# PSUM banks shared out by stage, an earlier end of the first batch's attention, and values loaded ahead of stores

## The chip, the cores and the metric

The kernel runs on one core of a Trainium2 chip. The metric is the device time of one execution in microseconds (us). Before the change three runs gave a median of 913.34 us (911.04 to 914.92).

## The reference

Three parts follow one another. q, k and v have 4 batches, 8 heads, 576 tokens and 64 dimensions. Per head there are two attentions, and their results are added: one over q, k, v averaged over groups of 4 tokens (144 by 144 scores), one over the full sequence in which a token sees only tokens nearer than 4.

```python
q_d, k_d, v_d = (t.reshape(B, H, 144, 4, D).mean(axis=3) for t in (q, k, v))
out_d = softmax(scale * q_d @ k_d.T) @ v_d
local = where(abs(i - j) < 4, scale * q @ k.T, -1e9)
x = repeat(out_d, 4) + softmax(local) @ v      # 2304 tokens x 512
h = x @ w_in                                   # 512 -> 2048
x = (h * sigmoid(1.702 * h)) @ w_out           # 2048 -> 512
out = ((x @ w1) * (x @ w2)) @ w3 @ w_out2      # 512 -> 1024 -> 1024 -> 512
```

## The kernel before

The large weights are loaded as 64-bit numbers and decoded to fp32 on VectorE (DVE; L176, L179 and L182) and ScalarE (ACT, L169). Every large product is made of three TensorE (PE) matmuls on a high and a low half of each operand (`mm3`, L120 to L123); the halves are made by `split` (L113 to L115: ACT writes the high half, DVE or GpSimd (POOL) the low one).

**First stage (0 to about 122 us).** w3 times w_out2 is computed once, so that the second half of the model needs one product less. There are 16 steps (two halves by 8 row tiles). Step s has a w3 tile, decoded, transposed by four PE transposes (`w34_transpose`, L624) into the one bank of the PSUM pool `psh`, and copied out of it as `w3t` by ACT (L626) and DVE (L627); then `w34_mm` issues 12 matmuls into four accumulators `ps_w34` (pool `psy`, four banks). The transposes of step s + 2 are issued ahead of the matmuls of step s.

**Attention.** A pair of heads is one unit n, 4 units a batch; here it is called a head. It has pieces: T (transposes of q and k, L286), S (scores: local ones L332, averaged ones L367, then the softmax on DVE, ACT and POOL), P (transposes of the probabilities, L417) and V (products with v, L446 and L459, then `v_pool` L452 and `v_local` L467, which adds both and stores x to DRAM, `x_d`, L471). Batch 0's pieces are woven into the first stage and batch b + 1's into block b of what follows. `att_pieces` writes the list of pieces with a gap behind each; `Pump` hands out a piece when the gap has been counted down, one count per call, and a call stands behind every `mm3` of the first stage. Banks for T, S, P and the V parts come from the pool `pst`, three banks. The softmax of batch 0 has its exps on ACT, 12 to a head (L317).

**Blocks.** The 2304 tokens go in five blocks (512, 512, 512, 256, 512 tokens). At a block's start x is read back from `x_d` (`tok_load`, L648) in four pieces and split (`tok_split`, `x_t`, L114 and L115). Then 16 steps `h_step` (12 matmuls into `ps_h`, the activation L676, a split) and `y_step` (12 matmuls into `ps_y`). The four heads of the last batch take another way for their local attention, on DVE and POOL (`l_scores` and others, L504 and on), woven into the blocks too. From the fourth block on no attention is left.

**What sets the order.** Each engine works through its own queue in order, and the order in the queue is made ahead of time by a scheduler from issue order, priorities and dependencies. `tc.issue_after(x)` only says that an instruction stands behind x in that order: an attention piece stands behind the `mm3` that came before it in the program (L609, `done["mm"]`), and may be put later. SP and ACT also issue the DMAs, each in the order of its queue.

## Time and profile before

| what | value |
|---|---|
| median of three runs | 913.34 us |
| profiled execution | 912.47 us, span 910.7 us, so 1.77 us lie outside the span |
| PE busy | 848.9 us, 93% |
| DVE busy | 598.4 us, 66% |
| ACT busy | 385.2 us, 42% |
| POOL busy | 149.6 us, 16% |

The span is the time from the first to the last instruction. Busy time is the sum in which an engine had an instruction under way; an idle time is printed in brackets behind the instruction in front of which it lies, with what ended it. In the timelines start times are microseconds from the span's start, and "x4" behind an instruction stands for four in a row. The granted clock is 1.00 for 2.4 GHz; 0.50 would be 1.2 GHz throughout.

### The profile page before, as it was taken

To read this page: it belongs to the slowest core of one execution; us is meant where nothing else is said; L and a number is where in the kernel's file an instruction comes from. 1 tells how busy PE (TensorE), PEld (TensorE's weight loads), DVE (VectorE), ACT (ScalarE), POOL (GpSimd) and SP (SyncE) were. 2 spreads that over 40 slices of the span, in tenths; PEclk is the share of its full clock that TensorE was granted. 3 is DMA by queue.
4 is the path that set the end of the run, shared out by engine and by line. 5 is a ranking of instruction groups with operands and counts; after the bars stand their busy time and mean duration, and the time that the engine had idled before them with its cause. 6 is when DMAs were issued, how large, how long until landed. Compare 5 with 4: busy or idle time off the path is not lost.

```text
span 910.7 us, 13574 instructions
## 1 busy us (share of the span) xinstructions
PE 848.9 (93%) x5132; PEld 721.9 (79%) x5132; DVE 598.4 (66%) x1061; ACT 385.2 (42%) x748; POOL 149.6 (16%) x153
## 2 busy tenths in 40 slices
PE   4497977999988999989999999999999999999998
PEld 3375865887756877767788998888999899989996
DVE  5896668898779999694446795333545554555451
ACT  4575655776534545343345665333111411141111
POOL 6642433432223432310000000000000000000000
PEclk9798987999998989989999999999999999999999
DMA  8865674665653443443334999601555455545521
GB/s 239 251 196 151 190 205 148 181 184 147 155 173 80 88 96 99 107 112 59 80 115 151 355 309 355 220 0 47 200 205 207 175 193 211 206 176 187 217 81 70
DMA packets 140598, 150.76 MB, mean 166 GB/s; under 512 B 86898, under 2 KB 121460, under 8 KB 136436
## 3 DMA queue, kind: packets, MB, share of 16 engines
q1 hardware_dynamic: 119424, 141.21, 47.9%
q10 hardware_dynamic: 21108, 8.69, 3.9%
q8 instruction: 40, 0.66, 0.3%
q14 instruction: 26, 0.21, 0.1%
HBM read 117.75 MB, written 32.11 MB: 165 GB/s over the span
## 4 chain that ended last, share of the span: by engine, by line
PE 60%; DVE 1%; ACT 1%; POOL 0%; issue 0%; ACTq 0%
PE ps_ab L123 6%; PE ps_ab L121 6%; PE ps_ab L122 6%; PE ps_y L121 5%; PE ps_y L122 5%; PE ps_y L123 5%; PE ps_h L121 5%; PE ps_h L122 5%; PE ps_h L123 5%; PE ps_o L122 4%; PE ps_o L123 4%; PE ps_o L121 4%; PE ps_pt L417 1%; PE ps_sp L367 0%; PE ps_v L459 0%; PE ps_vp L446 0%
## 5 line engine op out<-in xcount | busy, mean ns | idle before, releaser
L121 PE MATMUL ps_h<-x_t,w 128*128 128x512 f32 (+1 forms) x320 | 126.6, 395 | 14.6 <-ACT g_t L676 6.0
L122 PE MATMUL ps_h<-x_t,w 128*128 128x512 f32 (+1 forms) x320 | 123.3, 385 | 7.5 <-DVE x_t L115 7.4
L123 PE MATMUL ps_h<-x_t,w 128*128 128x512 f32 (+1 forms) x320 | 122.2, 382 | 0.0
L122 PE MATMUL ps_y<-gl,w 128*128 128x512 f32 (+1 forms) x320 | 118.9, 372 | 2.0 <-DVE gl L115 2.0
L121 PE MATMUL ps_y<-gh,w 128*128 128x512 f32 (+1 forms) x320 | 118.4, 375 | 0.0
L123 PE MATMUL ps_y<-gh,w 128*128 128x512 f32 (+1 forms) x320 | 118.2, 369 | 0.0
L123 PE MATMUL ps_ab<-b_t,a_in 128*128 128x384 f32 x336 | 112.5, 335 | 0.0
L121 PE MATMUL ps_ab<-b_t,a_in 128*128 128x384 f32 x336 | 112.5, 335 | 0.0
L122 PE MATMUL ps_ab<-b_t,a_in 128*128 128x384 f32 x336 | 112.4, 334 | 0.0
L115 DVE TENSOR_TENSOR gl<-g_t,gh 128x512 fp32r<-128x512 f32 (+1 forms) x80 | 56.7, 709 | 72.4 <-ACT gh L114 72.0
L676 ACT ACTIVATE g_t<-ps_h 128x512 f32<-128x512 f32 (+1 forms) x80 | 44.3, 554 | 130.8 <-PE ps_h L123 118.2
L121 PEld LDWEIGHTS ps_h<-x_t,w 128*128 128x128 f32 x320 | 62.4, 195 | 31.6 <-ACT g_t L676 9.9
L122 PEld LDWEIGHTS ps_h<-x_t,w 128*128 128x128 f32 x320 | 62.8, 196 | 18.6 <-DVE x_t L115 9.8
L123 PEld LDWEIGHTS ps_h<-x_t,w 128*128 128x128 f32 x320 | 62.8, 196 | 10.9
L114 ACT ACTIVATE abh<-ab 128x384 fp32r<-128x384 f32 x24 | 12.6, 526 | 137.2 <-DVE ab L801 137.2
L122 PEld LDWEIGHTS ps_y<-gl,w 128*128 128x128 f32 x320 | 60.4, 189 | 12.7 <-DVE gl L115 3.4
L121 PEld LDWEIGHTS ps_y<-gh,w 128*128 128x128 f32 x320 | 60.6, 189 | 11.0 <-issue 1.0
L123 PEld LDWEIGHTS ps_y<-gh,w 128*128 128x128 f32 x320 | 60.3, 189 | 10.0
L182 DVE SCALAR_TENSOR_TENSOR dec<-dec,st 128x512 int32<-128x512 int32 x72 | 58.1, 815 | 12.8 <-ACT dec L169 11.3
L121 PEld LDWEIGHTS ps_ab<-b_t,a_in 128*128 128x128 f32 x336 | 63.1, 188 | 0.9
L122 PEld LDWEIGHTS ps_ab<-b_t,a_in 128*128 128x128 f32 x336 | 63.1, 188 | 0.9
L123 PEld LDWEIGHTS ps_ab<-b_t,a_in 128*128 128x128 f32 x336 | 63.1, 188 | 0.0
(152 smaller groups left out, 1639.9 us busy)
## 6 DMA issues: line engine op xcount, KB each, us to landing
a_in<-a_d SPq DMA_DIRECT2D x24, 1792.0 KB
st<-in_moe_w_dram SPq DMA_DIRECT2D x32, 512.0 KB
a_d<-ap SPq DMA_DIRECT2D x8, 1792.0 KB
st<-in_moe_w_out_dram SPq DMA_DIRECT2D x24, 512.0 KB
st<-in_moe_w_in_dram SPq DMA_DIRECT2D x16, 512.0 KB
yr<-y_d SPq DMA_DIRECT2D x12, 384.0 KB
out_dram<-osb SPq DMA_DIRECT2D x17, 256.0 KB
s_v<-in_v_dram ACTq DMA_DIRECT2D x15, 288.0 KB
```

What stands on the lines that cost most here:

```text
L114: nc.scalar.activation(hi, raw, AF.Copy)
L115: lo_eng.tensor_tensor(lo, raw, f32(hi), op=ALU.subtract)
L121: nc.tensor.matmul(ps, ll, rh, start=start, stop=False, skip_group_check=more)
L122: nc.tensor.matmul(ps, lh, rl, start=False, stop=False, skip_group_check=more)
L123: done["mm"] = nc.tensor.matmul(ps, lh, rh, start=False, stop=stop, skip_group_check=more)
L182: nc.vector.scalar_tensor_tensor(t, t, 3, st[:, :, 0], op0=ALU.logical_shift_left, op1=ALU.bitwise_or)
L417: nc.tensor.transpose(ps[:, i - c0], src, ident)
L676: nc.scalar.activation(g[:, :n], ps[:, :n], AF.Gelu_apprx_sigmoid)
```

## The change

In the first stage `psh` gets two banks and `pst` two (one and three before); both pools are closed behind the stage and opened anew as `psh1` with one bank and `pst1` with three, which is what the blocks had before. In the first stage S is issued as two pieces, `s_near` (local scores, their reduction and exps) and then `s_far` (averaged scores); before, one piece had the averaged scores first. The gaps change: for batch 0 from 2 to 1 behind a piece, with a wait of 3 calls ahead of every V and 3 behind it; for later batches a wait of 6 ahead of every V and 10 behind it, where there were 16 behind V and 4 ahead of the last V alone. The rest of batch 0's attention and the first two loads of x from `x_d` are issued ahead of the 15th step's matmuls, and the rest of the loads and the splits ahead of the 16th's (before: all behind the 16th). In the blocks the `mm3` behind an attention piece is to stand behind that piece's last matmul. The loads of the next head's values (`vw`) are issued behind V's local matmuls, ahead of the two stores to `x_d`, where they stood behind them.

```diff
@@ -73,8 +73,10 @@
     dram = ctx.enter_context(tc.tile_pool(name="dram", bufs=1, space=DRAM))
     ldp = ctx.enter_context(tc.tile_pool(name="ldp", bufs=len(LOCAL), space=DRAM))
     psy = ctx.enter_context(tc.tile_pool(name="psy", bufs=1, space=PSUM))
-    psh = att_end.enter_context(tc.tile_pool(name="psh", bufs=1, space=PSUM))
-    pst = att_end.enter_context(tc.tile_pool(name="pst", bufs=3, space=PSUM))
+
+    ps_end = ctx.enter_context(ExitStack())
+    psh = ps_end.enter_context(tc.tile_pool(name="psh", bufs=2, space=PSUM))
+    pst = ps_end.enter_context(tc.tile_pool(name="pst", bufs=2, space=PSUM))
     x_d = dram.tile([128, KD, NT], F32, name="x_d")
     y_d = dram.tile([128, KD, NT], F32, name="y_d")
@@ -115,10 +117,12 @@
         lo_eng.tensor_tensor(lo, raw, f32(hi), op=ALU.subtract)
-    done = {"mm": None}
+    done = {"mm": None, "att": None, "strict": False}
     def mm3(ps, lh, ll, rh, rl, start, stop, more=False):
-        nc.tensor.matmul(ps, ll, rh, start=start, stop=False, skip_group_check=more)
+        att, done["att"] = done["att"], None
+        with tc.issue_after(att.ins) if att and done["strict"] else ExitStack():
+            nc.tensor.matmul(ps, ll, rh, start=start, stop=False, skip_group_check=more)
         nc.tensor.matmul(ps, lh, rl, start=False, stop=False, skip_group_check=more)
         done["mm"] = nc.tensor.matmul(ps, lh, rh, start=False, stop=stop, skip_group_check=more)
@@ -283,7 +287,7 @@
             halves = [pst.tile([128, FAC, UC], F32, tag="t", name="ps_t") for _ in range(2)]
             for c, ps in reversed(list(enumerate(halves))):
                 for r in range(FAC):
-                    nc.tensor.transpose(ps[:, r], st[:, c, r].rearrange("p h d -> p (h d)"), ident[:UC, :UC])
+                    done["att"] = nc.tensor.transpose(ps[:, r], st[:, c, r].rearrange("p h d -> p (h d)"), ident[:UC, :UC])
             for c, ps in enumerate(halves):
                 nc.scalar.activation(dst[:, c * UC:(c + 1) * UC].rearrange("p u r -> p r u"), ps, AF.Copy)
         if name == "q":
...
@@ -339,6 +343,19 @@
         nc.vector.tensor_reduce(at["mx", n][:, i0:i1], e[:, i0:i1], op=ALU.max, axis=X)
         if own_exp:
             s_exp(n, i0, i1, lambda i: e[:, i], SCALE)
+
+    def s_near(n, own_exp):
+        s_tiles(n, own_exp)
+        at["el", n] = att.tile([128, NQB, KW], F32, tag="el", name="el")
+        for i0, i1 in ((0, HQ), (HQ, NQB)):
+            ps = pst.tile([128, i1 - i0, KW], F32, tag="t", name="ps_s")
+            s_local_mm(n, i0, i1, ps)
+            s_local(n, i0, i1, own_exp, ps)
+
+    def s_far(n, own_exp):
+        s_pool(n, own_exp, s_pool_mm(n))
+        if n == 0:
+            v_means(0)
     def s_all(n, own_exp):
         s_tiles(n, own_exp)
@@ -355,8 +372,6 @@
         else:
             ps = s_pool_mm(n)
         s_pool(n, own_exp, ps)
-        if n == 0:
-            v_means(0)
     def s_pool_mm(n):
         kd = at["kd", n]
...
@@ -431,6 +446,8 @@
         ps = v_pool_mm(n, both[:, :SD])
         for i0, i1, pl in halves:
             v_local_mm(n, i0, i1, pl)
+        if n + 1 < B * HP and n + 1 not in LOCAL:
+            att_load_v(n + 1)
         v_pool(n, ps)
         for i0, i1, pl in halves[::-1]:
             v_local(n, i0, i1, pl)
...
@@ -469,8 +486,6 @@
             od[:, u0:u1].unsqueeze(2).to_broadcast([128, u1 - u0, FAC]), op=ALU.add)
         b, hp = divmod(n, HP)
         nc.sync.dma_start(out=x_d[:, hp, b * S + i0 * QB:b * S + i1 * QB], in_=xo)
-        if i1 == NQB and n + 1 < B * HP and n + 1 not in LOCAL:
-            att_load_v(n + 1)
     def l_load(n):
@@ -554,6 +569,8 @@
         if what == "T":
             return [lambda name=name: t_piece(n, name) for name in "qk"]
+        if what == "S" and n < HP:
+            return [lambda: s_near(n, own_exp), lambda: s_far(n, own_exp)]
         if what == "S":
             return [lambda: s_all(n, own_exp)]
         if what == "P":
@@ -562,32 +579,31 @@
             return [lambda: v_all(n), lambda: l_out(n, 0, HQ), lambda: l_out(n, HQ, NQB)]
         return [lambda: v_all(n)]
-    def att_pieces(b, own_exp, rest):
+    def att_pieces(b, own_exp):
         n0, out_ = b * HP, []
+        gap, wait, rest = (1, 3, 3) if b == 0 else (2, 6, 10)
         def add(n, what, gap):
-            fns = stage(n, what, own_exp)
-            out_.extend((fn, gap) for fn in fns)
+            out_.extend((fn, gap) for fn in stage(n, what, own_exp))
         if b == 0:
             add(n0, "T", 1)
-        add(n0, "S", 2)
-        add(n0 + 1, "T", 2)
-        out_.append((None, rest))
+        add(n0, "S", gap)
+        add(n0 + 1, "T", gap)
+        out_.append((None, wait + rest - 4))
         for i in range(HP):
             add(n0 + i, "P", 1)
             if i + 1 < HP:
-                add(n0 + i + 1, "S", 2)
+                add(n0 + i + 1, "S", gap)
                 if n0 + i + 2 < B * HP:
-                    add(n0 + i + 2, "T", 2)
-            else:
-                out_.append((None, 4))
-            add(n0 + i, "V", 2)
+                    add(n0 + i + 2, "T", gap)
+            out_.append((None, wait))
+            add(n0 + i, "V", gap)
             out_.append((None, rest))
         return out_
@@ -864,7 +880,7 @@
         jobs.size(2)
         jobs.decode(2)
         jobs.size(2)
-        pump = Pump(att_pieces(0, True, 6))
+        pump = Pump(att_pieces(0, True))
         w34_ready(0)
         pump.one()
         jobs.decode(2)
@@ -877,15 +893,22 @@
         for s, (half, j) in enumerate(steps):
             jobs.load(njobs(s + 4))
             w34_ready(s + 2)
+            if s == len(steps) - 2:
+
+                pump.drain()
+                tok_load(x_d, 0, 0)
+                tok_load(x_d, 0, 1)
+            elif s == len(steps) - 1:
+                tok_rest(x_d, 0)
             w34_mm(half, j, pump)
             jobs.decode(njobs(s + 2))
             jobs.size(njobs(s + 4))
-        pump.drain()
         early["pri"] = 100
-        tok_load(x_d, 0, 0)
-        tok_load(x_d, 0, 1)
         jobs.split(2)
-        tok_rest(x_d, 0)
+        done["strict"] = True
+        ps_end.close()
+        psh = att_end.enter_context(tc.tile_pool(name="psh1", bufs=1, space=PSUM))
+        pst = att_end.enter_context(tc.tile_pool(name="pst1", bufs=3, space=PSUM))
         def w34_load(f):
             t = g2p.tile([128, NB], F32, tag="xr", name="w34r")
@@ -920,7 +943,7 @@
         a_done = 0
         for j in range(nblk):
             last = j == nblk - 1
-            pump = Pump(att_pieces(j + 1, False, 16)) if j + 1 < B else Pump()
+            pump = Pump(att_pieces(j + 1, False)) if j + 1 < B else Pump()
             if j == nblk - 2:
                 jobs.split(2)
                 assert not jobs.jobs and not jobs.loaded and not jobs.sized and next(local, None) is None
```

The first place is PE's queue in the first stage, at the transposes of the fourth to sixth w3 tile. `ps_w<-ident,dec` are those transposes, `ps_w_297` to `ps_w_389` the four accumulators, `ps_t` is T, `ps_pt` is P, `ps_s` the local scores (the trace counts each matmul of S and V twice). Before:

```order
L122 MATMUL ps_w_389<-w,w3t 128x512
L123 MATMUL ps_w_389<-w,w3t 128x512
L624 MATMUL ps_w<-ident,dec 128x128 x4
L286 MATMUL ps_t<-ident,s_k 128x72 x4
L624 MATMUL ps_w<-ident,dec 128x128 x4
L121 MATMUL ps_w_297<-w,w3t 128x512
L122 MATMUL ps_w_297<-w,w3t 128x512
L123 MATMUL ps_w_297<-w,w3t 128x512
L417 MATMUL ps_pt<-ident,el 72x128 x8
L121 MATMUL ps_w_362<-w,w3t 128x512
```

After:

```order
L127 MATMUL ps_w_389<-w,w3t 128x512
L290 MATMUL ps_t<-ident,s_k 128x72 x8
L640 MATMUL ps_w<-ident,dec 128x128 x4
L432 MATMUL ps_pt<-ident,el 72x128 x8
L640 MATMUL ps_w<-ident,dec 128x128
L432 MATMUL ps_pt<-ident,ep 72x128 x3
L432 MATMUL ps_pt<-ident,el 72x128
L432 MATMUL ps_pt<-ident,ep 72x128 x3
L640 MATMUL ps_w<-ident,dec 128x128 x3
L336 MATMUL ps_s<-kT,qT 64x72 x18
L640 MATMUL ps_w<-ident,dec 128x128 x4
L125 MATMUL ps_w_297<-w,w3t 128x512
```

Behind the third step's matmuls stood the transposes of one w3 tile, four of T, and the transposes of the next tile; now eight of T, three tiles' transposes, all of P and the local scores of a head stand there, ahead of the fourth step's matmuls.

The second place is PE's queue at the end of the first stage, where `ps_v` is V of the batch's last head and `ps_h<-x_t` is the first work of block 0. Before:

```order
L122 MATMUL ps_w_970<-w,w3t 128x512
L123 MATMUL ps_w_970<-w,w3t 128x512
L417 MATMUL ps_pt<-ident,el 72x128
L417 MATMUL ps_pt<-ident,ep 72x128 x3
L446 MATMUL ps_v<-PT,vd 64x144 x2
L459 MATMUL ps_v<-PT,vw 64x64
L446 MATMUL ps_v<-PT,vd 64x144 x2
L459 MATMUL ps_v<-PT,vw 64x64 x17
L121 MATMUL ps_h<-x_t,w 128x512
L122 MATMUL ps_h<-x_t,w 128x512
L123 MATMUL ps_h<-x_t,w 128x512
```

After:

```order
L476 MATMUL ps_v<-PT,vw 64x64 x18
L127 MATMUL ps_w_1003<-w,w3t 128x512
L125 MATMUL ps_w_1020<-w,w3t 128x512
L126 MATMUL ps_w_1020<-w,w3t 128x512
L127 MATMUL ps_w_1020<-w,w3t 128x512
L125 MATMUL ps_w_1036<-w,w3t 128x512
L126 MATMUL ps_w_1036<-w,w3t 128x512
L127 MATMUL ps_w_1036<-w,w3t 128x512
L125 MATMUL ps_w_1080<-w,w3t 128x512
L126 MATMUL ps_w_1080<-w,w3t 128x512
L127 MATMUL ps_w_1080<-w,w3t 128x512
L125 MATMUL ps_h<-x_t,w 128x512
```

Before, V was the last work of the stage; now the last ten matmuls of the 16th step stand behind it.

The third place is DVE's queue at the start of block 1, around the splits `x_t<-xr`; `prod<-ql,kl` and `s` are the last batch's local attention, `el<-ps_s` to `el<-el,mx` the softmax of a head of batch 2. Before:

```order
L338 TENSOR_TENSOR el<-ps_s,band 128x360
L512 TENSOR_REDUCE r<-s 128x9
L339 TENSOR_REDUCE mx<-el 128x5
L513 TENSOR_TENSOR s<-s,r 128x63
L338 TENSOR_TENSOR el<-ps_s,band 128x288
L373 TENSOR_REDUCE mx<-ps_sp 128x3
L339 TENSOR_REDUCE mx<-el 128x4
L377 TENSOR_TENSOR ep<-ps_sp,mx 128x432
L515 TENSOR_REDUCE r<-s 128x9
L381 TENSOR_TENSOR el<-el,mx 128x648
L516 TENSOR_SCALAR r<-r 128x9
L115 TENSOR_TENSOR x_t<-xr,x_t 128x512
```

After:

```order
L117 TENSOR_TENSOR x_t<-xr,x_t 128x512
L521 TENSOR_REDUCE s<-prod 128x9
L117 TENSOR_TENSOR x_t<-xr,x_t 128x512
L526 TENSOR_TENSOR s<-s,near 128x63
L342 TENSOR_TENSOR el<-ps_s,band 128x360
L527 TENSOR_REDUCE r<-s 128x9
L343 TENSOR_REDUCE mx<-el 128x5
L528 TENSOR_TENSOR s<-s,r 128x63
L342 TENSOR_TENSOR el<-ps_s,band 128x288
L388 TENSOR_REDUCE mx<-ps_sp 128x3
L343 TENSOR_REDUCE mx<-el 128x4
L392 TENSOR_TENSOR ep<-ps_sp,mx 128x432
```

The block's last split stood behind seven instructions of a softmax, and stands ahead of them now.

## Rows read from the trace of the kernel before

**Rows 1.** Windows: length, busy of PE, PEld, DVE, ACT, POOL, clock, DMA.

```profile
23.00:46.00 23.00, 10.50 (x49) 8.20 (x49) 20.56 (x31) 12.20 (x37) 13.85 (x12) 0.70 0.81 250
46.00:69.00 23.00, 22.02 (x175) 17.51 (x174) 22.97 (x44) 17.69 (x49) 10.67 (x8) 0.93 0.60 189
69.00:92.00 23.00, 16.76 (x141) 13.22 (x140) 14.60 (x27) 13.02 (x42) 5.24 (x6) 0.85 0.56 164
...
138.00:161.00 23.00, 17.24 (x64) 13.19 (x64) 20.14 (x32) 13.82 (x24) 7.58 (x8) 0.78 0.45 140
...
391.00:414.00 23.00, 20.14 (x83) 14.89 (x84) 19.79 (x37) 10.58 (x17) 3.26 (x2) 0.85 0.51 129
414.00:437.00 23.00, 23.00 (x117) 18.31 (x117) 9.39 (x18) 9.09 (x14) 2.02 (x2) 1.00 0.28 53
```

**Rows 2.** Timeline of PE, 45 to 60 us: start, duration, instruction, idle before it.

```profile
45.10 1.12 PE L624 MATMUL ps_w<-ident,dec 128*128 128x128 f32 x4 [9.50 <-DVE w3t L627]
...
47.30 1.91 PE L417 MATMUL ps_pt<-ident,el 128*72 128x128 f32 x8
...
53.80 1.30 PE L332 MATMUL ps_s<-kT,qT 64*64 64x72 f32 x36
...
59.32 0.47 PE L286 MATMUL ps_t<-ident,s_q 72*128 72x72 f32 x4 [0.64 <-DVE el L338]
```

**Rows 3.** Timeline of DVE, 37 to 48 us.

```profile
37.45 1.49 DVE L176 TENSOR_SCALAR st<-st 128x512 int32<-128x512 int32 x1
...
47.32 0.42 DVE L176 TENSOR_SCALAR st<-st 128x512 int32<-128x512 int32 x1
```

**Rows 4.** Timeline of PE, 68 to 84 us.

```profile
70.15 0.39 PE L122 MATMUL ps_w<-w,w3t 128*128 128x512 f32 x1
70.38 0.39 PE L123 MATMUL ps_w<-w,w3t 128*128 128x512 f32 x1
...
74.94 0.66 PE L624 MATMUL ps_w<-ident,dec 128*128 128x128 f32 x4 [2.19 <-DVE w3t L627]
79.61 1.12 PE L624 MATMUL ps_w<-ident,dec 128*128 128x128 f32 x4 [4.01 <-DVE w3t L627]
...
83.47 0.95 PE L367 MATMUL ps_sp<-kd,qd 64*64 64x144 f32 x12
```

**Rows 5.** Timeline of DVE at 77.8 us.

```profile
77.80 0.43 DVE L176 TENSOR_SCALAR st<-st 128x512 int32<-128x512 int32 x1 [1.84 <-DMA st<-in_moe_w_in_dram]
```

**Rows 6.** Timeline of ACT, first and last of one head's 12 exps.

```profile
61.85 0.33 ACT L317 ACTIVATE el<-el,nb 128x72 f32<-128x72 f32 x1
...
66.43 0.37 ACT L317 ACTIVATE ep<-ps_sp,nb 128x144 f32<-128x144 f32 x1
```

**Rows 7.** Timeline of PE, 124 to 152 us.

```profile
124.49 1.22 PE L459 MATMUL ps_v<-PT,vw 72*64 72x64 f32 x34
...
143.57 0.80 PE L122 MATMUL ps_h<-x_t,w 128*128 128x512 f32 x1 [2.36 <-DVE x_t L115]
...
151.79 0.40 PE L121 MATMUL ps_y<-gh,w 128*128 128x512 f32 x1
```

**Rows 8.** Timeline of all engines, 131 to 143 us.

```profile
131.79 0.81 DVE L467 TENSOR_TENSOR xo<-ps_v,od 128x320 f32<-128x320 f32 x2
...
134.74 0.33 SPq L648 DMA_DIRECT2D xr<-x_d  x1
...
138.00 0.68 ACT L169 ACTIVATE dec<-st 128x512 f32<-128x512 f32 x1 [3.02 <-DMA st<-in_moe_w_out_dram]
...
140.02 0.64 ACT L114 ACTIVATE x_t<-xr 128x512 fp32r<-128x512 f32 x1
...
142.83 0.68 DVE L115 TENSOR_TENSOR x_t<-xr,x_t 128x512 fp32r<-128x512 f32 x1
```

**Rows 9.** Timeline of PE, 269 to 274 us.

```profile
269.74 0.50 PE L122 MATMUL ps_h<-x_t,w 128*128 128x512 f32 x1 [2.22 <-DVE x_t L115]
...
273.66 0.79 PE L121 MATMUL ps_h<-x_t,w 128*128 128x512 f32 x1 [1.59 <-ACT x_t L114]
```

More of the change, by code (lines that the diff above doesn't have):

```diff
@@ L331, in s_local_mm @@
                 p = slice(h * D, (h + 1) * D)
-                nc.tensor.matmul(
+                done["att"] = nc.tensor.matmul(
                     ps[p, i - i0], qT[p, i * QB:(i + 1) * QB], kT[p, w0:w0 + KW], start=True, stop=True)
@@ L366, in s_pool_mm @@
                 p = slice(h * D, (h + 1) * D)
-                nc.tensor.matmul(ps[p, j], qd[p, j * PB:j * PB + QB], kd[p], start=True, stop=True)
+                done["att"] = nc.tensor.matmul(ps[p, j], qd[p, j * PB:j * PB + QB], kd[p], start=True, stop=True)
         return ps
@@ L416, in p_piece @@
                     src = at["ep", n][:, j, kc * UC:(kc + 1) * UC]
-                nc.tensor.transpose(ps[:, i - c0], src, ident)
+                done["att"] = nc.tensor.transpose(ps[:, i - c0], src, ident)
         for c0, c1, ps in banks:
@@ L445, in v_pool_mm @@
                 i = NQB + kc * NPB - NPH
-                nc.tensor.matmul(
+                done["att"] = nc.tensor.matmul(
                     ps[p], vd[:, h, kc], PT[:, i:i + NPB, h * QB:h * QB + PB], start=kc == 0, stop=kc == 1)
@@ L458, in v_local_mm @@
                 p = slice(h * D, (h + 1) * D)
-                nc.tensor.matmul(
+                done["att"] = nc.tensor.matmul(
                     ps[p, (i - i0) * QB:(i - i0 + 1) * QB], vw[:, i - i0, h], at["PT", n, i // NPH][:, i % NPH, h * QB:(h + 1) * QB],
```

## The prediction

> **What bounds the kernel now.** The windows come first: from 414 us on PE is busy for 23.00 of 23 us in every window to the end of the blocks, at clock 1.00, so time can be won or lost only ahead of that [rows 1]. There four stretches stand out: 23 to 46, 69 to 92, 138 to 161 and 391 to 414 us, where PE is busy for 10.50, 16.76, 17.24 and 20.14 us; in the window between the first two it is DVE that is full, with 22.97 of 23 [rows 1]. So PE's timeline is read next, at those stretches, and beside it those of the engines that PE waits for. The reader is to see three kinds of wait. At 45.10, 74.94 and 79.61 us PE waits 9.50, 2.19 and 4.01 us in front of the transposes of a w3 tile, each time for `w3t` on DVE, which empties the one bank of `psh` [rows 2, 4]: 15.70 us. At the change from the first stage to block 0 the products of block 0 wait for the last quarter of x until 143.57 us, while V had begun its last matmuls at 124.49 and ended them at 125.71 us [rows 7]. At the change to block 1 the same happens again with 2.22 and 1.59 us [rows 9]. Behind such a wait the clock is at half: a group of four transposes takes 1.12 us at 79.61 and 0.66 at 74.94 [rows 4], and the windows show a granted clock of 0.70, 0.85 and 0.78 there [rows 1].
>
> **The second bank of psh.** The first wait is not simply removed, because PE has to wait for `w3t` again a few rows later, with the matmuls of the fourth step. What goes is the emptiness. By the order, all of P, a head's local scores and the sixth tile's transposes now lie ahead of those matmuls. P's first eight take 1.91 us, the local scores 1.30, a group of transposes 0.66 [rows 2, 4]: 3.9 us of work that would otherwise come later. Against that, the fourth tile's copy on DVE has the L176 and L179 of two more tiles ahead of it, four instructions; one L176 takes 0.42 us, and 1.49 in the stretch where POOL works beside it, busy for 13.85 of 23 us [rows 1, 3], so 1.7 to 6.0 us; I take 2.5, nearer the short one, since a part of the four would have fallen in the stretched time anyway. That is 1.4 us won (from 2.1 lost to 2.2 won). The second and third wait, 6.20 us, go, because the transposes now run three to four tiles ahead of the products; late next is DVE, which was full up to 69 us, and which itself stood still for 1.84 us at 77.80 behind a load [rows 5]. I leave 1.0 us for that. The 3.86 us of half clock from 79.61 to 83.47 [rows 4] give back half, 1.9. Together 1.4 + 5.2 + 1.9 = 8.5 us (0 to 10).
>
> **Two banks of pst where there were three.** Now the second half of a head's T needs the bank that the averaged scores hold until the last of their exps. The 12 exps of a head run on ACT from 61.85 to 66.80 us, 4.95 us, the averaged ones last [rows 6]. In PE's new order there are 18, 7 and 20 matmuls of the products between the scores and that half in the three later heads, 0.23 us apart as at 70.15 and 70.38 us [rows 4]: 4.1, 1.6 and 4.6 us of cover. So 0.9, 3.4 and 0.4 us are open, and as other work of ACT and DVE stands between, the whole could be 12; I take 4.0. The other side is 0, where the exps start as soon as the local scores are there, which are now first. P behind V waits in the same way for `xo`: only the second V is followed by P at once; ACT's copy and DVE's two adds behind V took 6.08 us at the end of the stage (125.71 to 131.79 [rows 7, 8]), of which DVE's other splits are the greater part; I take 2.5 for the three heads (0 to 6). The trace of before has one wait of this kind, 0.64 us at 59.32 in front of T [rows 2]. Sum -6.5 (0 to -18). The first stage as a whole then comes out 2.0 us earlier.
>
> **The end of the stage.** V ends, then ACT and DVE make `xo` (131.79), SP stores it and issues two loads of weights ahead of the read (134.74), ACT makes the high half (140.02), DVE the low one, which is done at 143.51 [rows 8]: 6.08 + 2.95 + 5.28 + 3.49 = 17.8 us from V's last matmul. The move of the drain ahead of the 15th step would leave 24 matmuls of products behind V; the order leaves ten, 2.3 us. In the chain the four splits ahead of `xo` stay, and so do the two loads of weights ahead of the read. ACT stood 3.02 us at a decode that waited for a load, ahead of the high half [rows 8]; that load now starts as much earlier as SP does, so it may go or stay. I take 4.5 + 2.95 + 4.0 + 2.5 = 14.0, 3.9 us shorter (0 to 8). The six loads of values, which SP now issues ahead of the stores, cost nothing as long as they are out before `xo` is there; that is SP's time beside V and 4.5 us of the chain. If they are not, the stores move back by what is left of them, at 0.33 us for an issue as at 134.74 [rows 8], 2.0 us. From 143.57 to 151.79 all matmuls are at half clock [rows 7], 8.2 us that could be 4.1; a shorter wait saves some of that, I take 1.0. Sum 2.3 + 3.9 + 1.0 = 7.2 us (0 to 13).
>
> **The blocks.** All four splits of x now stand ahead of the softmax at the start of block 1, and the same holds for block 2. The two waits of 2.22 and 1.59 us [rows 9] lose what that softmax took on DVE. I take 2.0 (0 to 5, with half clock behind them); for block 2, where the window lacks 2.86 us of PE [rows 1], 1.0 (-1 to 3). The rule that an `mm3` stands behind the last matmul of an attention piece keeps V together. It adds no wait by itself, but PE takes its queue in order, and what was moved aside when it was late now stands in front of everything. The price per head is not shown in the blocks, where such waits are absent; the nearest row is 0.64 us [rows 2], 7.7 us for twelve heads, and from the other side 0. Behind V there are now 10 calls instead of 16 and 6 ahead of it, which gives ACT's copies of P more time. I take -2.5.
>
> **The sum.** 8.5 - 6.5 + 7.2 + 2.0 + 1.0 - 2.5 = 9.7 us, against the profiled execution's 912.47 us (a span of 910.7 and 1.77 around it): 902.8. That execution lies 0.9 us under the median, so the median would be 903.7; I say 904. A measurement of this kernel tells 0.5%, some 4.6 us, from no change, so faster means under 908.8 and slower over 917.9.
>
> **Rivals.** *Nothing comes of it.* Up to 75 us DVE is the bound, 20.56 and 22.97 of 23 us busy [rows 1], and it does the same work as before; the second bank then buys no earlier `w3t`, and the later waits of T and P eat what the two other waits gave. With 8.5 cut to 4, the new waits at 8 and the rest as summed (7.7) the profile comes to 908.8, and with the end of the stage at a third of its 7.2 to 913.6. For it: DVE's windows, and the chain behind V, which keeps most of its links. Against it: DVE had air at 77.80 [rows 5]. I give 912. *All of it.* The clock stays up: half clock from 79.61 to 83.47 and 143.57 to 151.79 [rows 4, 7] is 12.1 us, worth 6.0, of which the sum counts 2.9; the new waits are covered (6.5 back); the median would then be 894. For it: the cover of 4.1 and 4.6 us for two of the heads. Against it: each wait that stays lowers the clock again. *Slower.* One mechanism, PE's order at T's second half: with two banks that half stands on PE's queue in front of the products until ACT has done all 12 exps, three times 4.95 us [rows 6] with nothing behind it able to pass, and each such stop is followed by half clock, as 4.01 us at 79.61 were by 3.86 us [rows 4], 1.9 lost. That is up to 20.5 us instead of the 6.5 counted; it takes more than the 8.5 and 7.7 us of the other terms and pushes V and the chain behind it back: 912.47 + 4.3 = 916.8 for the profile, 917.7 for the median, and 922.9 where the strict order costs 7.7 instead of 2.5. The kernel is slower than before from 16.2 us of new waits on, and by the bound from 20.8. For it: ACT is 17.69 of 23 us busy in 46 to 69 [rows 1]. Against it: the local exps can now start before the averaged scores are there.
>
> In the rows the clock is at half behind the long waits, 9.50 and 4.01 us [rows 2, 4], and at full level behind 2.19 us at 74.94 [rows 4]. The Trainium skill (TensorE: Matmul & The Clock Gate, section "A second HAM failure mode: psum-queue depth-cycling") states that short stops between groups of matmuls, from cycling through PSUM banks, make the clock swing too. By that the two banks of `pst` would keep the half clock that the removed waits give back; the sum without that 2.9 us would be 906.6. The same page (section "HAM oscillation — how this bites in real kernels") reports a kernel in which double-buffering PSUM gave no further gain; by that the first rival would hold, and here too the bank is only worth what DVE can deliver, which the window of 22.97 us bears out up to 69 us and that of 14.60 behind it does not [rows 1].
>
> **How the numbers follow.** The forecast (899 to 908.8) 0.42; all of it (under 899) 0.20; nothing 0.22; slower 0.16. So faster 0.62, same 0.22, slower 0.16. The range leaves out a quarter of the second case below 892 (0.05) and most of the slower one above 919 (0.13). The likeliest case's own range is 899 to 908.8.
>
> **What would show it.** In the profile after, the wait of 9.50 us should still be there in smaller parts, but in front of the products and not of transposes, and those of 2.19 and 4.01 gone; the window of 69 to 92 should have PE over 20. T's second half should show waits behind an exp of ACT, together 2 to 6 us. The last V should end near 121 us and `ps_h` run in full from about 135 instead of 143.57. I am wrong if the first `ps_y` comes later than 148 us, if waits for `xo` or exps pass 12 us, or if PE's loss between 161 and 414 us grows.

## The result, and the profile after

Four runs of the changed kernel have a median of 924.62 us (923.91 to 926.16), four of the kernel before beside them 913.42 (911.04 to 914.92): 1.2% slower, ratio 1.0127, 95% interval 1.0102 to 1.0153. The forecast was 904 in 892 to 919. The profiled execution took 926.16 us with a span of 924.4, 13.7 us more than before.

The windows of the kernel after (length, busy of PE, PEld, DVE, ACT, POOL, clock, DMA; compare [rows 1]):

```profile
23.00:46.00 23.00, 10.36 (x52) 8.03 (x52) 19.91 (x31) 13.02 (x40) 11.41 (x11) 0.83 0.73 222
...
69.00:92.00 23.00, 18.56 (x176) 14.38 (x178) 18.93 (x35) 14.04 (x43) 10.76 (x12) 0.95 0.55 155
92.00:115.00 23.00, 17.77 (x162) 13.15 (x159) 14.57 (x31) 15.64 (x46) 4.16 (x7) 0.98 0.66 188
115.00:138.00 23.00, 20.75 (x216) 16.98 (x215) 17.86 (x27) 12.09 (x24) 11.01 (x13) 1.00 0.73 201
...
391.00:414.00 23.00, 16.45 (x67) 12.74 (x68) 20.74 (x38) 13.00 (x20) 3.27 (x2) 0.85 0.47 122
...
552.00:575.00 23.00, 19.46 (x96) 15.82 (x95) 17.70 (x33) 13.53 (x27) 0.00 (x0) 1.00 0.97 370
```

Two windows of the kernel before that stand beside them:

```profile
92.00:115.00 23.00, 22.94 (x219) 18.54 (x217) 14.92 (x30) 14.69 (x45) 11.04 (x15) 1.00 0.67 183
115.00:138.00 23.00, 17.30 (x165) 13.31 (x163) 13.05 (x22) 11.48 (x22) 7.84 (x8) 0.85 0.74 216
```

Three things are to be seen. The first stage gained nothing in sum: 69 to 92 us has 1.8 us more of PE and 115 to 138 us 3.45 more, 92 to 115 us lost 5.2. The window at the start of block 2, 391 to 414, lost another 3.69. And 552 to 575 us, where PE had been full, lacks 3.54.

When the `h_step`s begin says where the time is lost. Each block has 16 steps, so h0 opens block 0, h32 block 2 and h64 the last block; the first column is the start before, in us, and the others are differences from it, worked out from the timelines of PE (e1 to e9 are the experiments below):

```
step  before   after    e1     e2     e3     e4     e6     e7     e9
h0    129.04   +1.76  +2.01  +2.54  +1.12  +2.84  +1.19  +4.07  +0.11
h16   264.24   +0.11  +3.31  +3.93  +5.11  +4.76  -0.20  +8.50  -2.10
h28   363.04   +1.26  +0.47  +4.84  +2.29  +2.24  +0.24  +5.10  -1.74
h32   395.14  +10.55  +1.81  +3.00 +11.84  +2.56  +0.48  +5.92  -1.50
h64   545.58  +10.35  +0.04  +6.02 +11.29  +4.57  +0.76  +7.52  -2.33
h68   561.93  +13.69  +3.41  +6.02 +14.67  +4.57  +5.29 +12.48  -2.33
```

Each column is one execution, and executions of one kernel lie apart: those of the kernel before took 909.10 to 918.30 us in all, and the columns of after, e2 and e7 are the longest of their sets (926.16, 918.59 and 924.92 us, with medians of 924.62, 914.50 and 921.25). So a jump inside a column can be read, its level hardly.

The changed kernel enters block 2's approach level with the one before (h28 +1.26) and loses 9.3 us by h32 and 3.3 between h64 and h68. Nothing changes after that.

**The loss at block 2.** ACT's timeline of the kernel after, 379 to 395 us. `l_soft` (L529) is the exp of the last batch's local attention, for its last head:

```profile
379.62 1.28 ACT L529 ACT_TABLE_LOAD   x1 [4.02 <-POOL vd L311]
392.55 0.26 ACT L529 ACTIVATE s<-s 128x63 f32<-128x63 f32 x1 [11.64 <-DVE s L528]
393.00 1.28 ACT L692 ACT_TABLE_LOAD   x1
394.30 0.60 ACT L692 ACTIVATE g_t<-ps_h 128x512 f32<-128x512 f32 x1
```

DVE's timeline of the kernel after, with what that exp waits for:

```profile
385.45 1.41 DVE L521 TENSOR_REDUCE s<-prod 128x9 f32<-128x576 f32 x2 [5.14 <-POOL prod L519]
...
392.29 0.22 DVE L528 TENSOR_TENSOR s<-s,r 128x63 f32<-128x63 f32 x1
```

PE's timeline of the kernel after:

```profile
394.95 0.80 PE L125 MATMUL ps_h<-x_t,w 128*128 128x512 f32 x1 [5.77 <-ACT g_t L692]
395.54 0.63 PE L126 MATMUL ps_h<-x_t,w 128*128 128x512 f32 x1
...
399.81 0.56 PE L127 MATMUL ps_h<-x_t,w 128*128 128x512 f32 x1
```

ACT's timeline of the kernel before:

```profile
378.79 0.60 ACT L676 ACTIVATE g_t<-ps_h 128x512 f32<-128x512 f32 x1 [4.95 <-POOL vd L307]
...
384.20 0.60 ACT L676 ACTIVATE g_t<-ps_h 128x512 f32<-128x512 f32 x1 [0.74 <-PE ps_h L123]
...
393.33 0.26 ACT L514 ACTIVATE s<-s 128x63 f32<-128x63 f32 x1
```

DVE's timeline of the kernel before, with the last of that exp's input:

```profile
392.96 0.21 DVE L513 TENSOR_TENSOR s<-s,r 128x63 f32<-128x63 f32 x1
```

The exp runs at about the same time in both, 392.55 and 393.33 us, because its scores on DVE and POOL are not ready sooner. Before, two activations `g_t` stand ahead of it on ACT; after, it stands ahead of them. ACT is then idle for 11.64 us with PE's work behind it in its queue, and PE waits 5.77 us for `g_t`. Twelve matmuls follow that take 0.63 instead of 0.39 us and begin 0.43 instead of 0.23 us apart [rows 4], some 2.5 us more for the twelve. Together that is 8.3 of the 9.3 us. All waits of PE for `g_t` came to 6.0 us before (longest 2.2) and 21.6 after:

```profile
PE ps_h L125 <- ACT g_t L692: 21.6, 10, 5.8
PE ps_w L640 <- DVE dec L186: 20.9, 4, 9.0
```

**The loss at the last block** is of the same kind. ACT's timeline of the kernel after:

```profile
557.38 1.06 ACT L116 ACTIVATE ap<-sums 128x1024 fp32r<-128x1024 f32 x1 [1.31 <-DVE sums L735]
558.34 0.65 ACT L173 ACTIVATE dec<-st 128x512 f32<-128x512 f32 x1
560.33 0.63 ACT L116 ACTIVATE ap<-dec 128x512 fp32r<-128x512 f32 x1 [1.34 <-DVE dec L186]
560.87 1.13 ACT L116 ACTIVATE x_t<-xr 128x512 fp32r<-128x512 f32 x2
```

ACT's timeline of the kernel before:

```profile
544.77 0.62 ACT L114 ACTIVATE x_t<-xr 128x512 fp32r<-128x512 f32 x1
...
545.55 0.62 ACT L114 ACTIVATE x_t<-xr 128x512 fp32r<-128x512 f32 x1
...
547.94 1.06 ACT L114 ACTIVATE ap<-sums 128x1024 fp32r<-128x1024 f32 x1 [1.49 <-DVE sums L719]
```

The second pair of splits of the block's x stood ahead of the preparation of a later product (`ap`) and now stands behind it and its waits for DVE. PE waits for it; its timeline in the kernel after:

```profile
561.53 0.73 PE L125 MATMUL ps_h<-x_t,w 128*128 128x512 f32 x2 [2.69 <-ACT x_t L116]
```

**The first stage.** PE's waits of the kernel after:

```profile
46.94 0.48 PE L640 MATMUL ps_w<-ident,dec 128*128 128x128 f32 x1 [8.61 <-DVE dec L186]
52.31 0.48 PE L125 MATMUL ps_w<-w,w3t 128*128 128x512 f32 x1
...
76.15 1.04 PE L432 MATMUL ps_pt<-ident,el 128*72 128x128 f32 x8 [1.92 <-DVE xo L484]
86.64 0.47 PE L290 MATMUL ps_t<-ident,s_q 72*128 72x72 f32 x4 [0.93 <-ACT ep L321]
...
100.92 0.50 PE L125 MATMUL ps_w<-w,w3t 128*128 128x512 f32 x1 [1.92 <-ACT w34s L654]
```

The 9.50 us in front of the fifth tile's transposes [rows 2] became 8.61, and DVE is named still, now for the decode of the tile (`dec`) where it was the emptying of the bank. Over the stage, PE's waits in front of `ps_w` add up to 27.9 us before (15.7 and 0.5 for `w3t`, 10.7 for `dec`, 1.1 for `w`) and 28.0 after (20.9 for `dec`, 4.0 and 1.0 for `w3t`, 2.1 for `w34s`); 9.0 of it lie in front of the kernel's first transposes in either. V of the last head ends at 128.46 us instead of 125.71, and the first `ps_y` comes at 151.86 [rows 7: 151.79].

These are single executions too. In the five profiles with the old first stage (before, e3, e7, e10, e15) V ends at 125.71 to 130.50 us and the waits on `ps_w` are 27.5 to 30.0 us; in the ten with the changed one (after, e1, e2, e4, e5, e6, e9, e11, e13, e14) it is 126.81 to 131.14 and 23.7 to 28.4 us. So V does not end earlier, and that it ends later is not shown. Some 3 us less of waits on `ps_w` may be real; the banks don't make them, since e8, the changed stage with the old banks, has 25.0.

### The profile page after: what moved, and what is told of

Its sections match the earlier page's. It is cut to its first block, busy times and chain, and to the rows that moved or that the text cites. A ratio compares the mean times of both kernels' runs of the same rounds, so it can differ in the third digit from the quotient of the medians.

```text
span 924.4 us, 13591 instructions
## 1 busy us (share of the span) xinstructions
PE 847.1 (92%) x5132; PEld 719.6 (78%) x5132; DVE 605.8 (66%) x1061; ACT 385.3 (42%) x750; POOL 147.6 (16%) x153
## 4 chain that ended last, share of the span: by engine, by line
PE 55%; DVE 9%; ACT 3%; issue 2%; DMA 2%; POOL 1%; DVEq 0%; POOLq 0%; ACTq 0%; SPq 0%
PE ps_ab L127 6%; PE ps_ab L125 6%; PE ps_ab L126 6%; PE ps_h L125 4%; PE ps_h L126 4%; PE ps_h L127 4%; PE ps_y L125 4%; PE ps_y L126 4%; PE ps_y L127 4%; PE ps_o L126 4%; PE ps_o L127 4%; PE ps_o L125 4%; DMA st<-in_moe_w_dram 1%; DVE prod L540 1%; ACT ap L116 1%
## 5 line engine op out<-in xcount | busy, mean ns | idle before, releaser
L125 PE MATMUL ps_h<-x_t,w 128*128 128x512 f32 (+1 forms) x320 | 125.7, 393 | 31.4 <-ACT g_t L692 21.6
L117 DVE TENSOR_TENSOR gl<-g_t,gh 128x512 fp32r<-128x512 f32 (+1 forms) x80 | 58.9, 738 | 70.3 <-ACT gh L116 60.4
L127 PEld LDWEIGHTS ps_h<-x_t,w 128*128 128x128 f32 x320 | 62.2, 194 | 10.7
L186 DVE SCALAR_TENSOR_TENSOR dec<-dec,st 128x512 int32<-128x512 int32 x72 | 54.7, 773 | 8.3 <-ACT dec L173 7.4
```

What stands on the lines that cost most here:

```text
L117: lo_eng.tensor_tensor(lo, raw, f32(hi), op=ALU.subtract)
L125: nc.tensor.matmul(ps, ll, rh, start=start, stop=False, skip_group_check=more)
L127: done["mm"] = nc.tensor.matmul(ps, lh, rh, start=False, stop=stop, skip_group_check=more)
L186: nc.vector.scalar_tensor_tensor(t, t, 3, st[:, :, 0], op0=ALU.logical_shift_left, op1=ALU.bitwise_or)
```

## The experiments

Theory: one queue order on ACT at each of two places makes the 11 us, and the first stage is bound by DVE's decode, so that banks don't help. Rivals: the first stage is itself slower; the strict rule (an `mm3` stands behind the last matmul of the attention piece ahead of it) makes PE stand at many small places; the loads of values hold up the stores. Where nothing else is said, an edit is against the changed kernel. A ratio is to runs of the kernel before that were taken beside (their medians are 912.39 to 913.46 us), with its 95% interval; "..." in a diff stands for lines left out.

**e1, without the strict rule**

```diff
-        done["strict"] = True
```

> The changed kernel (924.6 us) without the rule that an mm3 stands behind the last matmul of an attention piece. Theory: the rule and the new gaps of the blocks together put the exp of the last head's local softmax ahead of the last two activations of block 1 on ACT, which costs 9 us around 395 us; without the rule ACT's order has that exp behind the 32nd activation again, and the time is about 915 us (912 to 918), with the wait of 5.77 us at 395 us gone. Rival (the two banks of the first stage and what follows from them are the loss): 922 to 926 us.

917.14 us (10 runs), ratio 1.0047, interval 1.0030 to 1.0064. The loss before h32 is gone (h28 +0.47, h32 +1.81), that of the last block is not (h64 +0.04, h68 +3.41).

**e2, with the old gaps for the later batches**

```diff
-        gap, wait, rest = (1, 3, 3) if b == 0 else (2, 6, 10)
+        gap, wait, rest = (1, 3, 3) if b == 0 else (2, 0, 16)
...
```

> The changed kernel with the gaps of batches 1 to 3 as they were (16 calls behind V, 4 ahead of the last V); the first stage and the strict rule stay. Theory: the exp of the last local softmax goes behind the 32nd activation on ACT, and the splits of the last block's x stand singly ahead of other work as before, so both losses go: 911 to 915 us. Rival (first stage): 922 to 926 us.

914.50 us, ratio 1.0016, interval 0.9998 to 1.0034. Neither loss occurs: the column has no jump at h32 or h68, and its level is that of the longest of ten executions. So of these runs the exp is put ahead of `g_t` only where the rule and the gaps come together (after, e3, e5, e12), and not with the gaps alone (e1, e7) or the rule alone (e2), while the last block's loss needs the gaps alone.

**e3, the blocks' part on the old first stage, and e4, the first stage's part on the old blocks.** e3 is the kernel before with the strict rule, the new gaps of later batches and the values ahead of the stores; e4 has the banks, the split of S, batch 0's gaps and the earlier drain, and leaves the values behind the stores as before:

```diff
 e3
+        gap, wait, rest = (2, 0, 6) if b == 0 else (2, 6, 10)
...
 e4
+        gap, wait, rest = (1, 3, 3) if b == 0 else (2, 0, 16)
...
```

> The kernel before with only what the change does in the blocks: strict rule, new gaps, loads of values ahead of stores. The first stage is the old one. Theory: ACT's order still has the exp of the last local softmax ahead of two activations, so the loss of 9 to 13 us is there: 921 to 927 us. Rival (first stage): 911 to 915 us.

> The kernel before with only what the change does in the first stage: two and two banks, scores in two pieces, gaps of batch 0, the drain and the loads of x ahead of the 15th step. Theory: the first stage gives nothing and takes little, 911 to 915 us (block 0 begins its products in full at 143 us as before). Rival (first stage is the loss): 921 to 927 us.

e3 took 927.17 us, ratio 1.0160 (1.0132 to 1.0187), with both losses; e4 took 918.68, ratio 1.0062 (1.0034 to 1.0089), with neither, between its two expectations, and is late by 2 to 5 us in every row of the table. The parts don't add: 13.7 and 5.2 us apart, 11.2 together.

**e5, the values behind the stores again**

```diff
-        if n + 1 < B * HP and n + 1 not in LOCAL:
-            att_load_v(n + 1)
         v_pool(n, ps)
...
         nc.sync.dma_start(out=x_d[:, hp, b * S + i0 * QB:b * S + i1 * QB], in_=xo)
+        if i1 == NQB and n + 1 < B * HP and n + 1 not in LOCAL:
+            att_load_v(n + 1)
```

> The changed kernel with the loads of values behind the stores to x_d, as before. Theory: the loads of values ahead of the stores cost SP 1 to 3 us at the end of the first stage, where the last store stood behind five of them (xo done at 130.9, stores at 131.9 and later); x would be complete 2 to 4 us earlier there (143.8 before), but the losses of 9 us at block 1 to 2 and 3.4 us at the last block stay: 920 to 924 us. Rival (the loads ahead of the stores make the loss at the start of block 2, where the stores waited 14 us behind them on SP): 914 to 917 us.

932.44 us, ratio 1.0211 (1.0176 to 1.0247): slower than the changed kernel, against both expectations. x is there 3.1 us earlier (PE goes on at 140.71 instead of 143.84), but on SP two loads of `w_in` that had gone out at 125.85 and 134.51 are issued at 137.70 and 142.64. SP's timeline of the kernel after, then of e5, for the first of the two:

```profile
125.85 0.38 SPq L149 DMA_DIRECT2D st<-in_moe_w_in_dram  x1
```

```profile
137.70 0.47 SPq L149 DMA_DIRECT2D st<-in_moe_w_in_dram  x1
```

DVE's and PE's timelines of e5:

```profile
152.31 0.43 DVE L180 TENSOR_SCALAR st<-st 128x512 int32<-128x512 int32 x1 [3.02 <-DMA st<-in_moe_w_in_dram]
```

```profile
154.72 0.50 PE L126 MATMUL ps_y<-gl,w 128*128 128x512 f32 x1 [4.26 <-DVE gl L117]
```

In block 0 it is the loads of the weights that come next behind x on SP. The loads of values thus have two sides. Ahead of the stores they hold up x: from V's last matmul to the last split of x it is 15.3 us in the kernel after, 9.5 in e5, 11.5 in e4 and 11.4 in e8, all three with the values behind. But they let the weights' loads follow earlier, which counts for more here. e4 bears the same mark: its second step begins 1.95 us earlier than before, its fifth 4.32 later, and between them DVE waits 1.70 us for a load of `w_in` (at 156.33) and PE 1.69 for `gl` (at 158.75). So e4's loss may well be that order and not the banks; e2, which has the values ahead and the strict rule too, took 914.50. No run here parts the two.

**e6, the exp moved.** As the changed kernel, with the exp of the last local head behind block 1's last activation on ACT, and six calls of time ahead of its softmax.

```diff
-        nc.scalar.activation(s, s, AF.Exp, scale=SCALE)
+        with tc.issue_after(done["g"].ins) if n == B * HP - 1 else ExitStack():
+            nc.scalar.activation(s, s, AF.Exp, scale=SCALE)
...
```

> The changed kernel with one thing more: the exp of the last head's local softmax is placed behind the last activation of block 1 on ACT. Theory: the 9 us at block 1 to 2 go, since ACT no longer holds the last activations behind an exp that waits for DVE and POOL: 915 to 917 us, and the wait of 5.77 us at 395 us is gone. Rival (the strict rule itself holds PE's order back there, by keeping V ahead of the last products): 922 to 926 us.

917.69 us (10 runs), ratio 1.0055 (1.0033 to 1.0077); h32 is at +0.48, h64 at +0.76 and h68 at +5.29. ACT's timeline of e6:

```profile
388.30 0.60 ACT L693 ACTIVATE g_t<-ps_h 128x512 f32<-128x512 f32 x1 [1.06 <-PE ps_h L127]
...
392.01 0.60 ACT L693 ACTIVATE g_t<-ps_h 128x512 f32<-128x512 f32 x1 [0.73 <-DVE xo L484]
...
393.92 0.26 ACT L530 ACTIVATE s<-s 128x63 f32<-128x63 f32 x1
```

The exp runs hardly later than in the changed kernel, at 393.92 for 392.55 us, but two activations no longer stand behind it. One instruction's place in ACT's queue is the first loss.

**e7, the gaps alone, and e8, e4 with the old banks**

```diff
 e7 (against before)
+        gap, wait, rest = (2, 0, 6) if b == 0 else (2, 6, 10)
...
 e8 (against e4)
-    psh = ps_end.enter_context(tc.tile_pool(name="psh", bufs=2, space=PSUM))
-    pst = ps_end.enter_context(tc.tile_pool(name="pst", bufs=2, space=PSUM))
+    psh = ps_end.enter_context(tc.tile_pool(name="psh", bufs=1, space=PSUM))
+    pst = ps_end.enter_context(tc.tile_pool(name="pst", bufs=3, space=PSUM))
```

> The kernel before with the new gaps of batches 1 to 3 alone. Theory: the exp stays behind the 32nd activation, so there is no loss at block 1 to 2, but the second pair of the last block's splits of x stands behind a decode on ACT, which costs 3.4 us at 560 us: 915.5 to 918.5 us. Rival (the gaps alone make both losses): 924 to 927 us.

> As the run with the first stage's part alone (918.7 us), but with one bank for psh and three for pst as before; the scores in two pieces, the gaps of batch 0 and the early drain stay. Theory: the banks gave and took about as much, since DVE's decode is what the transposes wait for (8.61 us at 47 us instead of 9.50), so the time stays at 916 to 921 us. Rival (the two banks of pst cost the 5 us): 911 to 915 us. A third outcome, over 923 us, would say that the second bank of psh carries a gain that the rest of the first stage's changes eats.

e7 took 921.25 us, ratio 1.0081 (1.0052 to 1.0110), more than expected: no loss ahead of h32, the one at the last block (h64 +7.52, h68 +12.48). Its column is at +4.07 at h0 already, ahead of the first new gap and behind a first stage that is the old one, and at +5.09 at h28; so most of the column's level at h28 belongs to this one execution, and a cost of the gaps in blocks 0 and 1 is not shown. The median, some 3 us above the forecast, stays unexplained. e8 took 917.23, ratio 1.0044 (1.0022 to 1.0066), which overlaps with e4: no difference between the banks can be told. e8 swaps both pools at once, so this alone would also fit a gain of one bank that the other eats; what speaks against that are the waits. PE's timeline of e8, with one bank in `psh` again:

```profile
47.50 1.11 PE L643 MATMUL ps_w<-ident,dec 128*128 128x128 f32 x4 [7.83 <-DVE w3t L646]
```

With one bank PE waits 7.83 us here for the bank to be emptied, with two 8.61 for the decode.

**e9, the exp moved and the old gaps for the last batch alone**

```diff
-        gap, wait, rest = (1, 3, 3) if b == 0 else (2, 6, 10)
+        gap, wait, rest = (1, 3, 3) if b == 0 else ((2, 0, 16) if b in (3,) else (2, 6, 10))
...
```

> The changed kernel with the exp moved (as in the run before it) and, besides, the old gaps for the last batch alone (16 calls behind V), which puts the second pair of the last block's splits of x singly ahead of other work on ACT again. Theory: both losses are then gone, and nothing else has been won or lost: 911.5 to 914.5 us, the same as the kernel before. Rival (the first stage and its end still cost some us that the two losses hid): 916 to 920 us.

912.42 us, ratio 0.9996 (0.9972 to 1.0020). Both losses are gone (no jump at h32, none at h68) and the time is that of before. Moving the exp gave back 6.9 us (924.6 to 917.7 in e6) and the old gaps of the last batch 5.3 more (917.7 to 912.4). Windows of e9:

```profile
391.00:414.00 23.00, 21.09 (x97) 16.26 (x98) 18.16 (x33) 13.00 (x20) 2.83 (x2) 1.00 0.58 142
552.00:575.00 23.00, 23.00 (x103) 19.04 (x102) 10.81 (x19) 9.58 (x16) 0.00 (x0) 1.00 0.96 353
```

**e10 and e11, x without its way through DRAM.** The last quarter of block 0's x is split straight from `xo`, in the kernel before (e10) and in e9 (e11):

```diff
+        if n == KD - 1:
...
+            split(xo[:, :c1 - c0], xh[hp][:, c0:c1], xl[hp][:, c0:c1], nc.vector)
...
```

> The kernel before, with the fourth piece of block 0's x split directly from xo in SBUF instead of from a copy that goes to x_d and back (the stores stay). Theory: the way through DRAM (store, read, 10.0 us from xo at 131.79 to the ACT split at 140.02 and the DVE split at 142.83) is what holds block 0's start; without it PE's waits of 3.50 and 2.36 us and some of the half clock behind them (8.2 us, half of it) go: 904 to 910 us. Rival (the weights of block 0 are late anyway): 911 to 914 us.

> As the run with the exp moved and the old gaps of the last batch, and with the fourth piece of block 0's x split directly from xo. Theory: with x no longer going through DRAM the earlier end of the attention can count: PE's waits of 5.82, 1.48 and 1.22 us around 141 us and part of the half clock go, 901 to 908 us, faster than the kernel before. Rival (the weights of block 0 are late): 910 to 914 us.

e10 took 915.41 us, ratio 1.0026 (1.0006 to 1.0045), e11 913.03, ratio 1.0001 (0.9980 to 1.0022): no gain, although PE has the whole x early; e10 lies above both of its expectations, e11 in its rival's range. PE's timelines of e10, then of e11:

```profile
140.54 0.40 PE L123 MATMUL ps_h<-x_t,w 128*128 128x512 f32 x1
148.37 0.79 PE L121 MATMUL ps_h<-x_t,w 128*128 128x512 f32 x1 [7.44 <-ACT g_t L681]
```

```profile
137.11 0.40 PE L127 MATMUL ps_h<-x_t,w 128*128 128x512 f32 x1
145.50 0.79 PE L125 MATMUL ps_h<-x_t,w 128*128 128x512 f32 x1 [8.00 <-ACT g_t L701]
```

ACT's timeline of e11 ahead of that `g_t`:

```profile
142.24 1.31 ACT L663 ACTIVATE w34s<-ps_w 128x512 f32<-128x512 f32 x2 [2.96 <-DMA w_d<-w34s]
143.56 1.28 ACT L701 ACT_TABLE_LOAD   x1
144.85 0.60 ACT L701 ACTIVATE g_t<-ps_h 128x512 f32<-128x512 f32 x1
```

It is ACT's order a third time: two copies that wait for a buffer's store stand ahead of `g_t` (in e10 two exps of a softmax and the table load).

**e12, less decoding.** As the changed kernel, but it leaves out the first two of the three DVE operations of the decode (L180, L183) for eight of w_out2's tiles.

```diff
+            sub2 = sts[1:] if len(sts) == 2 and skip[0] < 8 else sts
...
```

> The changed kernel without the two first DVE instructions of the decode for the eight w_out2 tiles of the first stage (16 instructions, 8.9 us; it leaves out that part of the decode). Theory: the wait that stands for the one in front of the transposes (8.61 us at 47 us, for a decode) is DVE's work, so it shrinks to 3 to 6 us and the fourth step's products begin at 46 to 50 us instead of 52.3. Rival (the wait is for a load or for a bank): 8 to 10 us and 51 to 53 us, as before.

One run, 924.38 us (no gain can be told). PE's timeline of e12:

```profile
43.79 0.48 PE L644 MATMUL ps_w<-ident,dec 128*128 128x128 f32 x1 [7.64 <-DVE dec L190]
...
49.45 0.63 PE L125 MATMUL ps_w<-w,w3t 128*128 128x512 f32 x1
```

The fifth tile's transposes come 3.15 us earlier and the fourth step 2.86, which is in the expected range. The ten other profiles with this first stage have these transposes between 46.53 and 47.69 us, so 43.79 is beyond what executions differ by, and DVE's decode does set that wait; it is still 7.64 us, more than the 3 to 6 expected.

**e13 to e15, ACT's queue at the start of block 0.** e13 is e9 with the last two copies `w34s` behind the first activation, and e14 is e11 with them behind the first split of `g_t`; e15 is e10 with the first softmax of the second batch three calls later, behind that activation.

```diff
 e13
...
+        while w34_late:
+            with tc.issue_after(done["g"].ins):
+                w34_late.pop(0)()
 e14
...
+        while w34_late:
+            with tc.issue_after(done["hi"].ins):
+                w34_late.pop(0)()
 e15
...
+        late = 3 if b == 1 else 0
+        if late:
+            out_.append((None, late))
...
```

> Edit: e9 (the softmax exp of the last local head moved, old gaps for the last batch) and, besides, the last two copies w34s of the first stage stand behind the first activation g_t of block 0 on ACT. Theory (x itself is late here, ACT's copies only come next): without direct x the products of the first step end near 143 us as before, so this edit alone brings nothing: 911.5 to 913.5 us, first g_t from 143.85 to 143 at the earliest. Rival (the copies and their stores are the bound of the start of block 0): g_t 2 to 3 us earlier and 909 to 911 us.

> Edit: e11 (e9 with the last quarter of x split straight from xo) and, besides, the last two copies w34s behind the first g_t and gh of block 0 on ACT. Theory (x was late, and once it is not, the first g_t is held on ACT's queue behind two copies that wait for their buffers' stores): the 8.00 us in front of the second step's products shrink to 3 to 5 us, the second step starts at 140.5 to 142.5 instead of 145.50, and 3 to 5 us of it stay to the end: 908 to 911 us. Rival (the weights of block 0 are late anyway): the wait moves to gl or w behind the second step, and the time stays at 912 to 914 us.

> Edit: e10 (before with the last quarter of x split straight from xo) and, besides, the scores and softmax of the second batch's first head are issued three calls later, so that their exps stand behind the first g_t on ACT. Theory (in-order ACT): the 7.44 us in front of the second step's products shrink to 1 to 3 us; a table load or two of 1.28 us come in later; 909 to 912 us, against 915.4 for e10 and 913.4 for before. Rival (DVE and the loads of the weights are the bound there): the wait moves to gl or w and the time stays at 914 to 917 us.

e13 took 913.21 us, ratio 0.9999 (0.9986 to 1.0012); e14 913.00, ratio 0.9999 (0.9986 to 1.0011); e15 913.47, ratio 1.0006 (0.9989 to 1.0023). e13 took what was expected, but its first `g_t` came later and not earlier, at 147.68 us, behind a split that waited 2.57 us for DVE's decode; e14 and e15 took more than their theories said. In e14 the second step starts at 141.25 us as expected, 4.25 earlier than in e11, and the gain is gone 15 us later. PE's timeline of e14, then DVE's:

```profile
141.25 0.80 PE L126 MATMUL ps_h<-x_t,w 128*128 128x512 f32 x1 [3.69 <-ACT g_t L708]
...
156.37 0.50 PE L127 MATMUL ps_y<-gl,w 128*128 128x512 f32 x1 [3.12 <-DVE gl L119]
```

```profile
154.69 0.43 DVE L181 TENSOR_SCALAR st<-st 128x512 int32<-128x512 int32 x1 [3.18 <-DMA st<-in_moe_w_in_dram]
```

DVE waits for a load of `w_in`, and `gl` stands behind its decode. So three things lie closely one behind the other there: x, ACT's order, and the weights. In e15 the 7.44 us are gone, and the 2 us that it won on e10 (its interval and e10's overlap) bring it level with before. No version here is faster than the kernel before beyond its interval.

## Why the prediction was wrong

- **The blocks** is the step that failed. Its three terms, +2.0, +1.0 and -2.5 us, come to a gain of 0.5; the runs show a loss of some 12. "It adds no wait by itself" and a price of 2.5 us, at most 7.7, were taken from PE's queue and PE's waits alone. The scheduler's new order also moved an exp on ACT ahead of two activations, and splits of x behind `ap`. e6 and e9 price these at 6.9 and 5.3 us. What would have shown it stood in ACT's queue, which was not read at block 2; a timeline row of before with the exp at 393.33 was enough to say when its scores are ready.
- "Time can be won or lost only ahead of" 414 us is wrong by the last block's loss. A full PE says that nothing can be won there; it says nothing on what can be lost. Ahead of it the prediction named four stretches and left out 253 to 276 us, where PE was busy for 17.67 of 23 us, less than the 20.14 of 391 to 414, though it counted the waits there.
- **The second bank of psh** brought nothing of its 8.5 us. The wait went from the bank to the decode behind it, DVE, as the first rival had it: 8.61 us for `dec` with two banks, 9.50 and in e8 7.83 for `w3t` with one, and e8's time against e4's. The waits of 2.19 and 4.01 us did go from the transposes, and smaller ones came at the products and in the attention. The 3.9 us of other work pulled ahead were seen (the order put them there) but the fourth step came 6.4 us later, not 2.5. The Trainium skill (TensorE: Matmul & The Clock Gate, section "HAM oscillation — how this bites in real kernels") reports a kernel in which double-buffering PSUM gave no further gain. These runs agree: e8 against e4 shows none that can be told.
- **Two banks of pst** held in size, and only in part by its mechanism. T waited 2.1 us for exps (4.0 forecast), 0.5 in e4, and not at all in e8 with three banks. P waited 2.7 us for `xo` (2.5 forecast), but in e8 it waits 3.0, so that number came out by luck: it is not the banks. A wait of 2.1 for `w34s` came besides. The slower rival's mechanism, T's second half, thus did not decide; that the kernel came out slower, as it said, has another cause.
- **The end of the stage** brought nothing of its 7.2 us. From V's last matmul to the last piece of x it was 15.3 us (14.0 forecast, 17.8 before), but V did not end earlier, where 2.3 us and the first stage's 2.0 were counted (128.46 us, for "near 121"). e10, e11 and e14 show that the gain of that chain would not have lasted: ACT's order and then the weights are next. The loads of values ahead of the stores, priced at 0 to 2 us of cost, cost that chain some 4 to 6 us (15.3 against 9.5 to 11.5) and are still worth about 8 us in all (e5: 932.4 against 924.6), it seems because the weights' loads follow earlier on SP; the edit also moves loads in the later blocks.
- The range missed because the unknown of a moved order was bounded by waits that PE already had. Two of the signs of being wrong that the prediction names did come: the first `ps_y` at 151.86 us, later than 148, and PE's loss between 161 and 414 us grew, from 14.6 to 26.3 us.

Open: whether the order of the values is the whole of e4's loss; why e7's median lies above its forecast; and what else holds e14 between 157 us and h8.

## What to carry to other kernels

Where a scheduler makes the order, read every engine's queue at each stage boundary before pricing a change, above all the activation engine's: an instruction whose input comes late, put ahead of one that the matmul engine needs, can cost that engine much of its wait (here 5.77 of ACT's 11.64 us, and 6.9 us of the kernel's time with what follows). Ask of a removed wait which resource stands right behind it, here the decode behind the bank and the weights behind x. A stretch in which the bounding engine is full has no gain in it, but it can still be spoilt.

## What the runs showed of the hardware

ACT loaded a table of functions (1.28 us) at every change between an exp and the activation `g_t`, 32 times in the kernel after. Around one exp of 0.26 us these loads stand at 379.62 and 393.00 us; the first of them ran early, while ACT waited for the exp's input, and cost nothing there. The twelve matmuls behind PE's stop of 5.77 us, 0.43 us apart, ran at the lower of the two clock levels, 1.2 of 2.4 GHz (the granted clock from 388.0 to 400.2 us is 0.72 on average, and 1.00 behind it); those behind a stop of 0.69 us in e6, 0.23 us apart, at the higher one (1.00 from 379 to 391 us).
